# Row scatters from a queue, row numbers of y in a tile of their own, and an earlier place for the w1 loads of the first large visits

## The chip, the cores and the metric

The kernel runs on one core of a Trainium2 chip. The metric is the time of one execution on the device in microseconds (us). The engines are PE (matrix multiplication), DVE (VectorE), ACT (ScalarE), POOL (GpSimd) and SP (here only an issuer of DMAs). The DMA engines work beside them: SP's loads go through one queue, POOL's scatters through another.

## The reference

The first part is a convolution over the sequence (8 sequences of 2880 tokens, 192 channels) whose 7 weights are different for every token and head; they are the softmax of `weight_gen`. The second part sends each of the 23,040 tokens to one of 16 experts (4 groups of 4, the largest logit of each) and scales the expert's output by both softmax weights.

```python
w = np.exp(weight_gen - weight_gen.max(-1, keepdims=True))
w = w / (w.sum(-1, keepdims=True) + 1e-09)            # [B, S, 8 heads, 7]
x = np.einsum('bshk,bskhg->bshg', w, x_unf).reshape(N, 192)
g_idx = argmax(x @ w_group)                            # group, gate g_w from its softmax
e_idx = argmax(x @ w_expert[g_idx])                    # expert, gate e_w from its softmax
out[token] = g_w * e_w * (relu(x @ w1[g, e]) @ w2[g, e])   # 192 -> 1024 -> 192
```

## The kernel before

The tokens lie as 128 partitions x 180 columns. Fifteen column groups (g0 to g14) of twelve columns each go through three steps. The softmax (lines 258 to 263, on DVE and ACT) and the convolution (DVE products, some of the sums on PE) make the rows `xrow`; the tiles `wt` and `xin` that they read are loaded by `load_group` (lines 115 and 125). The routing (`logits` and `ranks`) finds each token's expert and its place in the expert's list, `posi`. Then, per group, twelve indirect DMAs on POOL (lines 480 to 482 and 488) scatter 128 rows each of 194 numbers (192 channels, the gate and the token's own number) to `rows` in DRAM, where every expert has a stretch of its own.

The experts' work goes by visits. A visit takes rows of one expert: 128 (plain), 256 (pair) or 384 (triple). Its inputs are `xb` (the rows, line 744), w1 and w2 (`wc`, line 768), all asked by SP. The first ten visits are plain and use float32 w1 as it is (`wa`, line 755). All others are large: w1 comes into `raw` tiles (512 KB at line 757, and 256 KB each from w1 and from `w1lo` at line 764), and ACT casts it into `wa` (lines 781 and 790), with a subtraction on DVE (line 805). `prep_d` (825 to 830) and `prep_x` make the visit's transposed inputs; `gemm1` (872) and the relu on ACT (878, 883) make the hidden layer, `gemm2` (910) the output, ACT scales it to `y` (919), and POOL scatters y's 128 rows to `out` by the token's numbers, which it reads from `xb` (927). In this kernel a visit's DMA on POOL therefore holds its xb buffer until it is done.

Fifteen rounds of visits follow the groups: a round may begin when the groups that it needs are scattered (the table `ENDS`: 2, 3, ... 15 groups), and the last one holds most triples. DVE's work for the next groups is a generator that the loop over visits advances (`fill`), by a planner's clocks for each engine. The order on PE, ACT, DVE and SP is that in which the program is written; POOL's order is left to the scheduler (line 101):

```python
ctx.enter_context(tc.manual_schedule(engines={ET.PE, ET.Activation, ET.DVE, ET.SP}))
```

In the loop of `blocks`, the inputs of later visits are asked (lines 1074 to 1077) at the last unit of a visit.

Of the kernel before, what the change touches and what calls it, by code (L numbers as in the profile page):

```python
# [11 lines left out]
I32 = mybir.dt.int32  # L12
# [8 lines left out]
LATE = (1.0, 3.0, 3.0)  # L21
AHEAD = (1.0, 1.0, 2.5)
HURRY = 12
WHOLE = 13
SINGLE = tuple((k,) for k in range(7))
MIXED = ((0, 1), (2,), (3,), (4,), (5,), (6,))
# [11 lines left out]
def conv_moe_kernel(ctx: ExitStack, tc: tile.TileContext, x, wgen, w_group, w_expert, w1, w2, out):  # L38
    nc = tc.nc
# [157 lines left out]
    def ring(name, n, shape, dt=F32):  # L197
        tiles = [const.tile(shape, dt, name=f"{name}{i}") for i in range(n)]
        at = [0]

        def take(i=None):
            at[0] += 1
            return tiles[(at[0] if i is None else i) % n]
        return take
# [3 lines left out]
    new_xh = ring("xh", 2, [P, 2, 3 * P], F32R)  # L208
    new_xl = ring("xl", 2, [P, 2, 3 * P], F32R)
    new_y = ring("y", 9, [P, D])  # L210
    hls = []

    def new_hl():
# [6 lines left out]

    new_raw = [ring(f"raw{i}", m, [P, n]) for i, (n, m) in enumerate(((F, 2), (F, 2), (NFT * D, 1)))]

    state = {"slots": False, "open": False, "unit": 0, "starve": False, "ph": 0, "hold": False}

    def ph_tile(k, shape):
        return ps_h.tile(shape, F32, name=f"ph{k}")
# [9 lines left out]
    def run(eng, cost, *deps):  # L236
        clk[eng] = max([clk[eng]] + [d + HOP for d in deps]) + cost
        return clk[eng]
# [10 lines left out]
    def round_of(g):  # L249
        return next(r for r in range(NR) if g < ENDS[r])  # L250
# [164 lines left out]
    def ranks(g, o, ls, tls):  # L415
# [61 lines left out]
        pi = rt.tile([P, SG], I32, name="posi", bufs=2)[:, 0:n]  # L477
        nc.vector.scalar_tensor_tensor(out=pi, in0=ps, scalar=-1.0, in1=ps, op0=ALU.mult, op1=ALU.max)
        yield TINY
        for s in range(n):  # L480
            run("pool", 1.28, clk["dve"])
            scatter_row(pi[:, s:s + 1], xrow[s // SC][:, s % SC, :], round_of(g))
        if g + 1 in ENDS:
            yield from table(round_of(g))
        o.routed = True

    def scatter_row(idx, src, r):
        written_once(nc.gpsimd.indirect_dma_start(  # L488
            out=rows[:, :], out_offset=bass.IndirectOffsetOnAxis(ap=idx, axis=0),
            in_=src, in_offset=None, bounds_check=NROW - 1, oob_is_err=False), r)  # L490
# [109 lines left out]
        for h in range(2):  # L600
            nc.gpsimd.dma_start(out=rows[NROW + h * BK:NROW + (h + 1) * BK, :].rearrange("(p t) c -> p t c", t=2), in_=pad2)

    scoring, ranking = [], []
    slow = [[halves(), None]]

    def front():
        side = []
        set_up()
        load_group(1)
        next(slow[0][0])  # L610
        yield from softmax(0)

        def pace(g):
            return 99 if g <= FIRST else HURRY if g < MAIN + 3 else 8 if g in ENDS else 2

        def beside(g, n):
            rush = g >= FIRST and not grp[FIRST - 1].routed
            if g >= FIRST and not rush:
                for q in list(slow):
                    yield from move(slow, q, 1)  # L620
            for q in side[:1]:
                if not rush:
                    yield from move(side, q, 3)
            yield from routing(g)

        def routing(g):
            if ranking:
                yield from move(ranking, ranking[0], pace(g))
            if scoring and (not ranking or g < FIRST):
                yield from move(scoring, scoring[0], pace(g) if scoring[0][2].chunks == 2 or g >= FIRST - 1 else 3)  # L630

        def settle(g):
            while not grp[g].routed:
                qs = ranking or scoring
                q = qs[0]
                yield from move(qs, q, 99)
                if qs and qs[0] is q and q[1] is not None:
                    yield Until(q[1][1]) if q[1][0] == "time" else NEXT

        for g in range(ENDS[-1]):  # L640
            o = grp[g]
            o.routed = False
            scoring.append([logits(g, o), None, o])
            for n, c in enumerate(conv(g, o)):
                yield c
                if n == (2 if state["slots"] else 0) and 1 <= g < ENDS[-1] - 1:
                    load_group(g + 1)
                if n >= (12 if state["slots"] else 4) and not o.ahead and g + 1 < ENDS[-1] and g != FIRST - 1:
                    o.ahead = True
                    side.append([softmax(g + 1), None])  # L650
                yield from beside(g, n)
                if g == FIRST - 1 and n in (7, 8):
                    if n == 7:
                        soft = softmax(FIRST)
                    yield next(soft)
            if g == FIRST - 1:
                for n, c in enumerate(soft):
                    yield c
                    yield from beside(g, n)
            yield from finish_all(side)  # L660
            if g:
                yield from settle(g - 1)
        yield from settle(ENDS[-1] - 1)
# [54 lines left out]
    nmain = len(order)  # L718

    def ready(n):  # L720
        return order[n][:2] in arrive

    def plain(n):
        return order[n][1] == 1
# [98 lines left out]
        latest.clear()  # L823

    def prep_d(b):
        if b.plain:
            return
        b.xd = new_xd()[:, 0:b.nt]
        b.td = run("act", 0.1 + 0.13 * b.nt, b.o.tx)
        nc.scalar.copy(out=b.xd, in_=b.x[:, :, P:D].unsqueeze(2).broadcast_to([P, b.nt, 2, HP]))  # L830
# [92 lines left out]
    def send(b, t, y):  # L923
        if not b.o.whole:
            nc.vector.scalar_tensor_tensor(
                out=y, in0=b.py[t][:, D:2 * D], scalar=b.x[:, t, D:D + 1], in1=y, op0=ALU.mult, op1=ALU.add)
        ins = nc.gpsimd.indirect_dma_start(  # L927
            out=out[:, :], out_offset=bass.IndirectOffsetOnAxis(ap=b.x.bitcast(I32)[:, t, D + 1:D + 2], axis=0),
            in_=y, in_offset=None, bounds_check=NTOK - 1, oob_is_err=False)
        tc.declare_no_dep(ins.ins, group="outw", reason="every token is written once")  # L930
        tc.add_to_no_dep_group("outw", ins.ins)

    def need(n):
        while not ready(n):
            state["starve"] = True
            more = step() is not False
            assert more or ready(n)
        state["starve"] = False
# [13 lines left out]
    def blocks(n0, n1, paced):  # L952
# [92 lines left out]
        for i in range(len(units) + LAG):  # L1045
# [25 lines left out]
            if i < len(units):  # L1071
                n, at = units[i]
                end = at == last
                if end and n + 3 < n1 and (plain(n + 3) or plain(n + 2)):
                    ask_w(n + 3)
                    if not plain(n + 3):
                        ask_w(n + 4)
                did = 0
                for job in list(jobs):
                    m, part, h = job  # L1080
                    if m > n + 2 or (part == 3 and (m > n + 1 or at < LAG)):
                        continue
                    must = end and m == n + 1
                    if not must and (did >= 1 or (m, part) in want or not ready(m)):
                        continue
                    jobs.remove(job)
                    work_split(job)
                    did += 1
                state["unit"] += 1
            flush()  # L1090
            if paced:
                fill(clk["pe"] + AHEAD[0 if cur.plain else 1 if cur.o.whole else 2])
# [48 lines left out]
```

## Time and profile before

| | |
|---|---|
| median of 3 runs | 1333.68 us (1323.01 to 1336.16) |
| the profiled execution | 1335.81 us |
| its span, first to last instruction | 1334.1 us |
| mean granted TensorE clock | 0.951 of full speed |
| busy | PE 89%, DVE 71%, ACT 48%, POOL 34% |

The time of an execution holds a little more than the span. Busy time is that of an engine's instructions; idle time has behind it, in the timeline, the instruction that ended it. "issue" is time in which the engine waited for nothing that the profile shows, and "remote" is a semaphore whose setter the profile doesn't tell. PEclk is the granted clock in a stretch, as a share of full speed (2.4 GHz; its other level is 1.2 GHz).

### The profile page before, as it was taken

To read this page: it belongs to the slowest core of one execution; us is meant where nothing else is said; L and a number is where in the kernel's file an instruction comes from. 1 tells how busy PE (TensorE), PEld (TensorE's weight loads), DVE (VectorE), ACT (ScalarE), POOL (GpSimd) and SP (SyncE) were. 2 spreads that over 40 slices of the span, in tenths; PEclk is the share of its full clock that TensorE was granted. 3 is DMA by queue.
4 is the path that set the end of the run, shared out by engine and by line. 5 is a ranking of instruction groups with operands and counts; after the bars stand their busy time and mean duration, and the time that the engine had idled before them with its cause. 6 is when DMAs were issued, how large, how long until landed. Compare 5 with 4: busy or idle time off the path is not lost. (4 is left out here: it accounts for less than half of the span.)

```text
span 1334.1 us, 23736 instructions
## 1 busy us (share of the span) xinstructions
PE 1192.9 (89%) x8165; PEld 1104.5 (83%) x8165; DVE 950.5 (71%) x1660; ACT 640.1 (48%) x1232; POOL 455.6 (34%) x442
## 2 busy tenths in 40 slices
PE   5776877798999999999989798989786999999995
PEld 3444877688998989898989697989686999999995
DVE  8897776768988979798978597888633146655662
ACT  1223334344555555455545454645343466556652
POOL 6232331415253525344533415252416312112221
PEclk9988998788999999899999899999887999999998
DMA  9238789555878767677776666545436665565551
GB/s 258 85 120 275 239 213 287 190 197 172 265 224 278 215 236 225 228 223 253 229 237 213 217 196 209 188 155 168 158 88 216 197 205 149 154 176 165 151 164 39
DMA packets 78851, 261.94 MB, mean 196 GB/s; under 512 B 14669, under 2 KB 29559, under 8 KB 76928
## 3 DMA queue, kind: packets, MB, share of 16 engines
q1 hardware_dynamic: 59544, 220.85, 54.4%
q0 software_dynamic: 19056, 39.20, 8.8%
q8 instruction: 66, 1.08, 0.3%
q14 instruction: 65, 0.53, 0.1%
q10 hardware_dynamic: 120, 0.28, 0.1%
HBM read 216.92 MB, written 44.23 MB: 196 GB/s over the span
## 5 line engine op out<-in xcount | busy, mean ns | idle before, releaser
L872 PE MATMUL ph<-xh,wa 128*128 128x256 f32 (+1 forms) x1896 | 477.0, 321 | 8.1 <-issue 7.4
L910 PE MATMUL py<-wc,hh 128*128 128x192 f32 x2272 | 440.2, 334 | 34.4 <-issue 17.5
L927 POOL DMA_INDIRECT out<-y,xb x189 | 222.1, 1175 | 706.3 <-ACT y L919 449.5
L910 PEld LDWEIGHTS py<-wc,hh 128*128 128x128 f32 x2272 | 379.2, 196 | 40.6 <-issue 22.3
L872 PE MATMUL ph<-xl,wa 128*128 128x256 f32 (+1 forms) x1264 | 360.4, 300 | 8.1 <-issue 8.1
L878 ACT ACTIVATE hh<-ph 128x512 f32<-128x512 f32 (+2 forms) x320 | 175.9, 550 | 366.5 <-PE ph L872 258.4
L872 PEld LDWEIGHTS ph<-xh,wa 128*128 128x128 f32 x1896 | 329.5, 194 | 17.9 <-issue 16.4
L488 POOL DMA_INDIRECT rows<-xrow,posi x180 | 202.1, 1123 | 152.6 <-issue 65.9
L287 DVE TENSOR_TENSOR pr<-xin,wt 128x1152 f32<-128x1152 f32 x186 | 249.0, 1351 | 4.3 <-PE ph L328 2.0
L872 PEld LDWEIGHTS ph<-xl,wa 128*128 128x128 f32 x1264 | 243.4, 193 | 9.5 <-issue 9.5
L305 DVE TENSOR_TENSOR xrow<-xrow,pr 128x1152 f32<-128x1152 f32 x144 | 194.9, 1353 | 0.6
L805 DVE TENSOR_TENSOR wa<-raw,wa 128x1024 fp32r<-128x1024 f32 x79 | 96.5, 1221 | 127.8 <-ACT wa L781 111.7
L805 DVE SCALAR_TENSOR_TENSOR pr<-ph,hh 128x384 fp32r<-128x384 f32 (+1 forms) x120 | 68.8, 574 | 89.0 <-ACT hh L883 84.0
L805 DVE TENSOR_TENSOR xl<-tpx,xh 128x512 fp32r<-128x512 f32 (+1 forms) x99 | 62.8, 634 | 61.5 <-ACT xh L852 50.6
L883 ACT ACTIVATE hh<-ph 128x384 fp32r<-128x384 f32 (+1 forms) x120 | 61.1, 510 | 79.8 <-PE ph L872 70.5
L912 PE MATMUL py<-wc,hh 128*128 128x384 f32 x272 | 87.2, 362 | 0.0
L781 ACT CAST wa<-raw 128x1024 fp32r<-128x1024 f32 x79 | 82.9, 1049 | 7.0 <-DMA raw<-in_moe_w 7.0
L790 ACT CAST wa<-raw 128x1024 fp32r<-128x1024 f32 x79 | 82.8, 1048 | 0.5 <-DMA raw<-w1lo 0.5
L919 ACT ACTIVATE y<-py,xb 128x192 f32<-128x192 f32 x176 | 66.2, 424 | 27.2 <-PE py L910 19.0
L391 ACT COPY xT<-tp 128x384 f32<-128x384 f32 x84 | 40.3, 480 | 78.3 <-PE pl L367 30.5
L913 PE MATMUL py<-wc,pr 128*128 128x192 f32 x272 | 68.4, 251 | 0.0
L852 ACT CAST xh<-tpx 128x512 fp32r<-128x512 f32 (+1 forms) x99 | 53.5, 540 | 3.9 <-PE py L910 1.8
(170 smaller groups left out, 1287.2 us busy)
## 6 DMA issues: line engine op xcount, KB each, us to landing
wc<-in_moe_w SPq DMA_DIRECT2D x73, 768.0 KB
raw<-in_moe_w SPq DMA_DIRECT2D x79, 512.0 KB
xin<-in_x SPq DMA_DIRECT2D x14, 1728.0 KB
raw<-in_moe_w SPq DMA_DIRECT2D x87, 256.0 KB
raw<-w1lo SPq DMA_DIRECT2D x79, 256.0 KB
raw<-in_moe_w SPq DMA_DIRECT2D x17, 768.0 KB
xb<-rows SPq DMA_DIRECT2D x59, 194.0 KB
wa<-in_moe_w SPq DMA_DIRECT2D x22, 384.0 KB
```

The lines of the kernel that those rows point to most:

```text
L287: nc.vector.tensor_tensor(out=dst, in0=o.xin[:, c0 + k:c0 + k + SC, :].rearrange("p s (h g) -> p s h g", g=HG), in1=w4[:, c0:c0 + SC, :, k ...
L305: nc.vector.tensor_tensor(out=acc, in0=acc, in1=prs[k - 2], op=ALU.add)
L488: written_once(nc.gpsimd.indirect_dma_start(out=rows[:, :], out_offset=bass.IndirectOffsetOnAxis(ap=idx, axis=0), in_=src, in_offset=None, ...
L781: nc.scalar.copy(out=o.wa[:, 0, :], in_=o.raw[0])
L790: nc.scalar.copy(out=o.wa[:, 2, :], in_=o.raw[1])
L805: f(*a, **k)
L872: nc.tensor.matmul(ph[:, v, :], lhsT=w[:, f0:f0 + P], rhs=rhs, start=i == 0, stop=i == len(terms) - 1)
L878: nc.scalar.activation(out=hh, in_=ph, func=AF.Relu)
L910: nc.tensor.matmul(b.acc[t], lhsT=hh[:, v, c], rhs=wc[0][:, f, :], start=f == 0 and not (b.wide and t == 1), stop=f == NFT - 1 and not (b. ...
L912: nc.tensor.matmul(b.py[t], lhsT=hh[:, v, c], rhs=wc[f // 4][:, f % 4].rearrange("p l d -> p (l d)"), start=f == 0, stop=False)
L913: nc.tensor.matmul(b.acc[t], lhsT=hl[:, v, c], rhs=wc[f // 4][:, f % 4, 0, :], start=False, stop=f == NFT - 1)
L927: ins = nc.gpsimd.indirect_dma_start(out=out[:, :], out_offset=bass.IndirectOffsetOnAxis(ap=b.x.bitcast(I32)[:, t, D + 1:D + 2], axis=0), ...
```

## The change

Three things are changed.

*The scatters of rows.* `ranks` no longer issues them, but puts them into a list, `sending`. `send_rows` takes them from it, and for the first groups does so at once. Otherwise the loop over visits issues one in each unit, if the planner's clock for PE is 3 us further (`send_due`). A group's rows are issued at the latest when the next but one is begun. A round counts as ready only when the rows of its groups are sent.

*The row numbers of y.* In `prep_d`, ACT copies the token's numbers of a visit from xb to a ring of six small tiles, `ids`, and the y scatter reads them from there.

*The asks of w1.* Of the first two large visits, w1 is asked two visits sooner.

```diff
+    new_ids = ring("ids", 6, [P, 3, 1], I32)
...
-        for s in range(n):
-            run("pool", 1.28, clk["dve"])
-            scatter_row(pi[:, s:s + 1], xrow[s // SC][:, s % SC, :], round_of(g))
+        sending.extend((g, pi[:, s:s + 1], xrow[s // SC][:, s % SC, :], s == n - 1, clk["dve"]) for s in range(n))
+        if g < FIRST:
+            send_rows()
...
+    def send_rows(most=99):
+        while sending and most > 0:
+            g, idx, src, end, at = sending.pop(0)
+            run("pool", 1.28, at)
+            scatter_row(idx, src, round_of(g))
+            most -= 1
+            if end:
+                state["sent"] = g + 1
+                for r, nb in arrive:
+                    if ENDS[r] == g + 1:
+                        arrive[r, nb] = max(arrive[r, nb], clk["pool"] + 7.0)
+    def send_due():
+        if sending and state["due"] <= clk["pe"]:
+            send_rows(1)
+            state["due"] = max(state["due"], clk["pe"] - 2.6) + GAP
...
         for g in range(ENDS[-1]):
+            while sending and sending[0][0] < g - 1:
+                send_rows(1)
...
-        return order[n][:2] in arrive
+        return order[n][:2] in arrive and state["sent"] >= ENDS[order[n][0]]
...
     def prep_d(b):
+        b.ids = new_ids()[:, 0:b.nt]
+        nc.scalar.copy(out=b.ids, in_=b.x.bitcast(I32)[:, :, D + 1:D + 2])
+        run("act", 0.22, b.o.tx)
...
-            out=out[:, :], out_offset=bass.IndirectOffsetOnAxis(ap=b.x.bitcast(I32)[:, t, D + 1:D + 2], axis=0),
+            out=out[:, :], out_offset=bass.IndirectOffsetOnAxis(ap=b.ids[:, t, :], axis=0),
...
-                if end and n + 3 < n1 and (plain(n + 3) or plain(n + 2)):
+                if end and n + 3 < n1 and plain(n + 3):
                     ask_w(n + 3)
-                    if not plain(n + 3):
-                        ask_w(n + 4)
+                if end and n + 6 < n1 and plain(n + 4) and not plain(n + 5):
+                    ask_w(n + 5)
+                    ask_w(n + 6)
...
+            send_due()
             flush()
```

POOL's order around the rows of one middle group, g11 (its row tiles are the `xrow` and `posi` here), before:

```order
L927 DMA out_0<-y7_188,xb2_174 23040x192
L927 DMA out_0<-y8_189,xb2_174 23040x192
L488 DMA rows_89<-xrow_7677,posi_9184 188928x194 x6
L488 DMA rows_89<-xrow_7678,posi_9184 188928x194 x6
L927 DMA out_0<-y0_181,xb0_172 23040x192
L927 DMA out_0<-y1_182,xb0_172 23040x192
```

The same group with the change:

```order
L951 DMA out_0<-y8_189,ids0_190 23040x192
L507 DMA rows_89<-xrow_7788,posi_9294 188928x194 x6
L507 DMA rows_89<-xrow_7789,posi_9294 188928x194 x4
L951 DMA out_0<-y0_181,ids1_191 23040x192
L951 DMA out_0<-y1_182,ids1_191 23040x192
L507 DMA rows_89<-xrow_7789,posi_9294 188928x194 x2
L951 DMA out_0<-y2_183,ids2_192 23040x192
```

The twelve scatters of the group are still in a row up to the tenth; two y scatters stand ahead of the last two. Of the thirteen groups from g2 on, g3, g6 and g8 are cut 7 and 5, g9 and g11 10 and 2, the others but the last not at all.

POOL's order at the last group, g14, before (line 541 loads a place for a padding block):

```order
L488 DMA rows_89<-xrow_10371,posi_11394 188928x194
L927 DMA out_0<-y0_181,xb2_174 23040x192
L927 DMA out_0<-y1_182,xb2_174 23040x192
L488 DMA rows_89<-xrow_10371,posi_11394 188928x194 x5
L488 DMA rows_89<-xrow_10372,posi_11394 188928x194 x6
L541 TENSOR_LOAD pfi_11471
```

With the change, in two pieces, the first up to the padding blocks and the second behind the last of them:

```order
L507 DMA rows_89<-xrow_10469,posi_11567 188928x194 x2
L951 DMA out_0<-y2_183,ids1_191 23040x192
L951 DMA out_0<-y3_184,ids1_191 23040x192
L507 DMA rows_89<-xrow_10469,posi_11567 188928x194 x3
L560 TENSOR_LOAD pfi_11614
```

```order
L562 DMA rows_89<-pad_169 256x1x194
L507 DMA rows_89<-xrow_10469,posi_11567 188928x194
L507 DMA rows_89<-xrow_10470,posi_11567 188928x194 x6
L951 DMA out_0<-y6_187,ids3_193 23040x192
L951 DMA out_0<-y7_188,ids3_193 23040x192
```

Seven of the twelve scatters now stand behind the sixteen padding blocks, among which (not shown) two more y scatters stand behind the seventh.

SP's order where the plain visits end, before (`wt` and `xin` are the next column group's, `xb0` and `wc` the last plain visit's, `raw00` is the first part of w1 of the first large visit; TENSOR_LOAD and ISA rows read and compute addresses):

```order
L115 DMA wt_1734<-in_weight_gen 128x672
L125 DMA xin_1736<-in_x 128x3456
L743 TENSOR_LOAD tab1_782
L743 ISA x2
L744 ISA
L744 DMA xb0_172<-rows_89 128x194
L768 ISA
L768 DMA wc_1808<-in_moe_w2 128x1536
L752 TENSOR_LOAD tab2_1382
L752 ISA x2
L757 ISA
L757 DMA raw00_190<-in_moe_w1 128x1024
```

With the change, from the second large visit's `raw` on:

```order
L778 DMA raw01_197<-in_moe_w1 128x1024
L785 ISA
L785 DMA raw11_199<-in_moe_w1 64x1024
L785 ISA
L785 DMA raw11_199<-w1lo_90 64x1024
L116 DMA wt_1773<-in_weight_gen 128x672
L126 DMA xin_1775<-in_x 128x3456
L764 TENSOR_LOAD tab1_788
L764 ISA x2
L765 ISA
L765 DMA xb0_172<-rows_89 128x194
L789 ISA
```

All six raw loads of two visits stood behind `wc` and now stand ahead of `wt`; `xb0` and `wc` keep their place behind `xin`.

## Rows read from the trace of the kernel before

**Rows 1.** Busy line of the page; windows: us, busy (x count) per engine, PEclk, DMA, GB/s.

```profile
PE 1192.9 (89%) x8165; PEld 1104.5 (83%) x8165; DVE 950.5 (71%) x1660; ACT 640.1 (48%) x1232; POOL 455.6 (34%) x442
...
231.00:1040.00 809.00, 742.49 (x5349) 705.99 (x5348) 619.26 (x1115) 405.55 (x765) 318.26 (x282) 0.95 0.66 209
1040.00:1330.00 290.00, 279.62 (x1843) 273.07 (x1841) 149.27 (x251) 166.76 (x322) 60.77 (x59) 0.99 0.53 154
0.00:231.00 231.00, 170.81 (x977) 125.46 (x978) 181.95 (x295) 67.81 (x146) 76.60 (x102) 0.93 0.71 211
```

**Rows 2.** Windows of 28 us around twelve runs of scatters: two, and the sum.

```profile
726.00:754.00 28.00, 19.11 (x121) 17.84 (x120) 14.70 (x29) 9.88 (x20) 16.18 (x16) 0.82 0.51 157
...
996.00:1024.00 28.00, 17.88 (x102) 16.56 (x101) 12.43 (x63) 7.45 (x14) 19.79 (x21) 0.77 0.54 168
sum 336.00, PE 276.08 PEld 255.85 DVE 244.41 ACT 144.64 POOL 212.46; mean PE 23.01 PEld 21.32 DVE 20.37 ACT 12.05 POOL 17.70
```

**Rows 3.** Twelve windows of 28 us between the runs: one, and the sum.

```profile
756.00:784.00 28.00, 28.00 (x241) 26.74 (x240) 25.24 (x32) 16.57 (x31) 4.73 (x4) 1.00 0.80 269
...
sum 336.00, PE 335.42 PEld 324.61 DVE 255.08 ACT 199.29 POOL 71.20; mean PE 27.95 PEld 27.05 DVE 21.26 ACT 16.61 POOL 5.93
```

**Rows 4.** Timeline of POOL: start, us, engine line op out<-in xcount [idle before <-releaser].

```profile
726.14 0.97 POOL L488 DMA_INDIRECT rows<-xrow,posi  x1 [5.89 <-DVE units L514]
...
740.23 0.97 POOL L488 DMA_INDIRECT rows<-xrow,posi  x1 [0.30 <-issue]
...
751.18 1.86 POOL L927 DMA_INDIRECT out<-y,xb  x1 [7.41 <-ACT y L919]
```

**Rows 5.** Timeline of PE and ACT at that run; ACT's waits over the span.

```profile
740.55 0.48 PE L910 MATMUL py<-wc,hh 128*128 128x192 f32 x1 [1.65 <-issue]
...
746.29 1.09 ACT L878 ACTIVATE hh<-ph 128x512 f32<-128x512 f32 x2 [15.24 <-remote]
...
ACT hh L878 <- remote: 76.9, 14, 15.2
```

**Rows 6.** Waits from 840 to 1100: us in total, times, longest.

```profile
SPq L744 <- DMA out<-y,xb: 140.6, 14, 25.7
...
ACT xd L830 <- DMA xb<-rows: 7.2, 6, 1.6
...
PE tpx L846 <- DMA xb<-rows: 3.4, 3, 3.0
```

**Rows 7.** Smallest ACT operation of the routing: durations in ns, min/median/max.

```profile
L345 ACT ACTIVATE exe<-de x15: 233/240/243, 50.2 to 993.2; 128x48 f32<-128x48 f32 x15
```

**Rows 8.** Timeline of SP's queue where the plain visits end.

```profile
194.98 0.38 SPq L115 DMA_DIRECT2D wt<-in_weight_gen  x1
...
198.35 0.33 SPq L757 DMA_DIRECT2D raw<-in_moe_w  x1
```

**Rows 9.** Timelines of DVE, ACT and PE behind these loads.

```profile
204.59 0.85 DVE L258 TENSOR_REDUCE m<-wt 128x96 f32<-128x672 f32 x1 [5.79 <-DMA wt<-in_weight_gen]
...
206.37 0.76 ACT L261 ACTIVATE wt<-wt 128x672 f32<-128x672 f32 x1 [1.54 <-DVE wt L260]
207.04 0.64 ACT L878 ACTIVATE hh<-ph 128x256 f32<-128x256 f32 x2
...
216.06 1.04 ACT L781 CAST wa<-raw 128x1024 fp32r<-128x1024 f32 x1 [7.02 <-DMA raw<-in_moe_w]
...
218.01 1.65 PE L910 MATMUL py<-wc,hh 128*128 128x192 f32 x4 [6.08 <-ACT y L919]
```

**Rows 10.** Windows over the same stretch.

```profile
204.00:210.00 6.00, 6.00 (x47) 5.77 (x48) 5.30 (x7) 2.05 (x5) 0.00 (x0) 1.00 1.02 373
210.00:216.00 6.00, 1.93 (x16) 1.74 (x14) 2.81 (x10) 0.00 (x0) 0.00 (x0) 1.00 1.03 202
216.00:226.00 10.00, 7.99 (x44) 7.99 (x45) 6.61 (x14) 6.11 (x14) 0.97 (x1) 0.66 1.03 275
```

More of the change, by code (lines that the diff above doesn't have):

```diff
@@ L23 @@
 HURRY = 12
+GAP = 3.0
 WHOLE = 13
@@ L221, in conv_moe_kernel @@
     new_raw = [ring(f"raw{i}", m, [P, n]) for i, (n, m) in enumerate(((F, 2), (F, 2), (NFT * D, 1)))]
-    state = {"slots": False, "open": False, "unit": 0, "starve": False, "ph": 0, "hold": False}
+    state = {"slots": False, "open": False, "unit": 0, "starve": False, "ph": 0, "hold": False, "sent": 0, "due": 0.0}
     def ph_tile(k, shape):
@@ L601, in set_up @@
             nc.gpsimd.dma_start(out=rows[NROW + h * BK:NROW + (h + 1) * BK, :].rearrange("(p t) c -> p t c", t=2), in_=pad2)
-    scoring, ranking = [], []
+    scoring, ranking, sending = [], [], []
     slow = [[halves(), None]]
@@ L934, in need @@
         while not ready(n):
+            send_rows()
+            if ready(n):
+                break
             state["starve"] = True
```

## The prediction

> **What bounds the kernel now.** I read the busy times first. PE works 1192.9 us of 1334.1 [rows 1], so 141 us of its time are open, and no other engine comes near it. Then I read the windows, to see where these 141 us lie. Up to 231 us PE has 170.81 us of work, which leaves 60.2 us open while the first rows are made and the plain visits run; from 231 to 1040 it has 742.49 of 809, which leaves 66.5; behind 1040 it has 279.62 of 290 [rows 1]. The middle stretch holds almost all that can be won: 66.5 us of idle time and a granted clock of 0.95, which is another 0.05 x 809 = 40 us of full-speed work.
>
> The middle stretch is not evenly loose. I cut twelve windows of 28 us around the runs of twelve row scatters and twelve of the same length between them. The calm ones have 335.42 us of PE work in 336, the ones with a run have 276.08 [rows 2, 3]. So the runs cost 335.42 - 276.08 = 59.3 of the 66.5 us, and the clock falls in them too (0.82 and 0.77 in two of the worst, 1.00 in a calm one). That is 59.3 / 12 = 4.9 us of idle time and 40 / 12 = 3.3 us of clock for each run.
>
> The timeline shows how a run does it. POOL issues twelve scatters 1.28 us apart, from 726.14 to 740.23 [rows 4]. Towards its end PE's matmuls come one by one with 1.65 us between them and wait for nothing that the profile names ("issue"), and ACT stands 15.24 us for a "remote" semaphore before the next relu [rows 5]; over the span ACT stands so 76.9 us in 14 places [rows 5]. It is not the bandwidth: the DMA share is 0.51 and 0.54 in two of the worst windows and 0.80 in the calm one [rows 2, 3]. What exactly is starved in PE's supply the trace does not tell; that it follows the runs of scatters it tells in every one of the twelve windows.
>
> **The change part by part.**
>
> **a) Scatters from a queue.** Issued one by one with 3 us between them, they would take the twelve back-to-back issues apart, which is where 59.3 + 40 = 99.3 us lie. But POOL's order is not the order in which the program is written: it is left to the scheduler, and the rows of the order show the scatters in runs again. Seven of the thirteen groups from g2 on still stand as twelve in a row; g3, g6 and g8 are cut 7 and 5, g9 and g11 10 and 2, each by two y scatters. Nothing in POOL's new program waits for the 3 us: no new wait is on a scatter. A cut alone is worth little, because the last group was cut 1 and 11 before and its window (996 to 1024) is the worst of all, with 28 - 17.88 = 10.1 us idle and 0.23 x 28 = 6.4 us of clock [rows 2]. So I put the twelve earlier groups at 0. Only the last group is truly taken apart: 2, then 3, then seven of the padding blocks, two y scatters, the other nine padding blocks, and the last 7. For it I take half of 10.1 + 6.4 = 16.5, which is **-8**. Bounds: 0, if the last 7 scatters cost what twelve did, and -99 if all runs were really thinned.
>
> **b) Row numbers for y in a tile of their own.** The y scatters no longer read xb, so a load into an xb buffer need not wait for them. SP stood 140.6 us for this in 14 places between 840 and 1100 [rows 6], which looks large, but SP is asked far ahead: in the same stretch PE waits 3.4 us for rows and ACT 7.2 [rows 6]. I take PE's **-3.4**; bounds 0 (the rows' scatters may be what is late next, since the load waits for those as well) and -3.4 - 7.2 = -10.6.
>
> **c) The copies.** One copy of at most 128 x 3 numbers for each of 90 visits on ACT. No copy so small stands in the trace; the nearest row is an activation of 128 x 48 at 0.240 us [rows 7], so at most 90 x 0.240 = 21.6 us of an engine that works 640.1 of 1334.1 us [rows 1]. They lie in front of the copy for the next visit that ACT does anyhow, with one visit of time ahead of them. Only in the plain stage does the copy stand a little earlier than the one that waited for xb, and there a relu is queued behind it. I take **+2**, a tenth; bounds 0 and +21.6 (if ACT's relus were always the last thing PE waits for, which rows 3 speak against: PE is full there).
>
> **d) w1 of the first large visits.** The order shows six w1 loads, 2 x (512 + 256 + 256) KB = 2.10 MB, moved ahead of wt and xin of the next column group, and ahead of xb and w2 of the last plain visit. SP issues them only from about 195 instead of 198.35 [rows 8]; the DMA engines have a share above 1.0 from 204 to 216 [rows 10], so this is an exchange of places in a full queue and not a gain of two visits. What comes sooner: before, ACT stood for raw to 216.06, and PE for 6.08 us behind that, until 218.01 [rows 9]. What comes later: wt, which landed at 204.59 and then released the softmax's maximum on DVE [rows 9]. Behind it are exp on ACT at 206.37 and, in ACT's order, the plain relu at 207.04 [rows 9]. With 2.10 MB ahead, at the 202 GB/s of the stretch in which mostly w1 arrived [rows 10], wt lands 10.4 us later, at 215.0, and the relu goes at 217.4 instead of 207.04. PE's stand of 6.08 us moves from behind to ahead of it and grows: 10.4 - 6.1 = **+4.3**. Bounds: -9.5, if the stand simply goes (6.1 us, and 0.34 x 10 = 3.4 us of the clock of 0.66 from 216 to 226 [rows 10]), and +10.4 if the old stand stays too.
>
> The sign of d) rests on who is served first. wt was asked at 194.98 and had landed by 204.59, raw was asked at 198.35 and landed by 216.06 [rows 8, 9]: in the order of asking. The Trainium skill (page DMA: Bandwidth & Descriptors, section Queues, rings and completion order) says that on each DMA engine the descriptors of a ring are consumed in ring order, while completions need not follow it. By that rule alone the exchange costs +4.3 and the forecast's sum holds; were transfers of one queue served side by side, it would be near -9.5.
>
> **Sum**, against the profiled execution of 1335.8: -8 - 3.4 + 2 + 4.3 = -5.1, which gives 1330.7. The median of the runs shown is 1333.7, 2.1 lower, so the forecast is **1329**.
>
> **The rivals.**
>
> *The runs are thinned after all.* Where a y scatter stands in a run, POOL stops for that y: 7.41 us in one place [rows 4]. If such stops let PE's supply recover in the cut groups, and later emission pulls the others apart too, half of the 99.3 us comes back: 1335.8 - 49.7 - 3.4 + 2 + 4.3 = 1289.0, as a median 1287. For it: the calm windows. Against it: seven groups uncut, and the cut last group of before being the worst. 0.16.
>
> *The w1 wait goes and the last run costs nothing.* 1335.8 - 9.5 - 16.5 - 3.4 + 2 = 1308.4, as a median 1306. For it: the stand behind raw is the largest single one at that place. Against it: wt, whose delay must then be hidden, though a relu is queued behind its exp. 0.18.
>
> *Slower: ACT stands behind wt.* The six loads hold wt back by 10.4 us, and the stand behind w1 does not go away, since w2 and xb of the last plain visit come behind xin: 128 x 3456 numbers, 1.77 MB, at 202 instead of 373 GB/s [rows 10] is another 8.8 - 4.7 = 4.1 us; PE then stands twice, which costs the half clock of 216 to 226 once more, 3.4; the last run costs what it did. 1335.8 + 10.4 + 4.1 + 3.4 + 2 - 3.4 = 1352.3, as a median 1350. It decides if wt lands behind about 215 with the relu queued behind its exp. For it: the DMA share above 1.0. Against it: DVE and ACT may have other work there, as PE had (6.00 of 6 us from 204 to 210). 0.18.
>
> *The change does nothing that can be seen*: scatters in runs, SP's waits hidden, the exchange of places neutral: 1334. It is one of the cases within 1%.
>
> **How the numbers follow.** A measurement of this kernel can tell about 1% from no change, that is 1320 to 1347. The forecast has 0.33 and the case of no effect 0.15, both within: same 0.48. Faster is 0.16 + 0.18 = 0.34, slower 0.18. The range reaches down to 1300, which takes in the second rival and leaves out most of the first, and up to 1351, which takes in the slower one: about 0.8 is inside. The forecast's own range, within its bounds, is 1320 to 1340.
>
> **What would show it.** a) In the profile after, the windows around runs of scatters should have the same 23.0 us of PE in 28 as before, with "issue" ahead of the matmuls, and only the last run less idle time; if the runs are still twelve long and PE is full in them, the link between runs and idle time is wrong. b) SP's waits for "out" should be gone and PE's waits for rows below 4 us. c) 90 copies of about 0.2 us, with PE's work in calm windows unchanged. d) wt should land near 215 and the plain relu near 217, and ACT should no longer stand for raw. A median under 1320 would say that the runs or the w1 wait went; one above 1347 that d) was mis-sized.

## The result and the profile after

The changed kernel takes 1347.85 us (median of 15 runs, 1333.14 to 1351.99), the kernel before beside it 1330.58 us (15 runs, 1323.01 to 1336.16). The ratio is 1.0118, with an interval of 1.009 to 1.0147: some 16 us slower by the ratio and 17.3 by the medians, where 1329 us and no change beyond 1% were forecast. The time lies in the stated range, and on the wrong side of before.

The profiled execution of after has a span of 1347.8 us, 13.7 more than before. The busy line of its page and two windows (in us: length, busy time and count of PE, PEld, DVE, ACT and POOL, then the granted clock, the DMA share and GB/s), as in [rows 1]:

```profile
PE 1189.4 (88%) x8165; PEld 1104.6 (82%) x8165; DVE 948.5 (70%) x1660; ACT 648.9 (48%) x1322; POOL 444.7 (33%) x442
...
0.00:231.00 231.00, 170.67 (x940) 124.06 (x941) 176.41 (x281) 66.67 (x153) 70.23 (x101) 0.90 0.66 203
231.00:1040.00 809.00, 728.63 (x5333) 696.99 (x5332) 621.17 (x1119) 410.16 (x822) 297.81 (x263) 0.94 0.65 206
```

PE works 3.5 us less than before and stands 1347.8 - 1189.4 = 158.4 us, against 141.2 [rows 1]: 17.2 more, and 17.2 - 3.5 is the 13.7 of the span. Up to 231 us the idle time is the same (60.3 us open, 60.2 before), but PE has done 940 matmuls where it had done 977, at a clock of 0.90 instead of 0.93, and the same y scatter starts 4.9 us later (the first line is before, the second after):

```profile
227.04 0.97 POOL L927 DMA_INDIRECT out<-y,xb  x1 [7.83 <-ACT y L919]
231.96 1.15 POOL L951 DMA_INDIRECT out<-y,ids  x1 [5.64 <-ACT y L943]
```

By 293 us most of this delay is gone: ACT's y there goes at 293.56, 1.8 us behind the 291.79 of before. From 231 to 1040 PE stands 80.4 instead of 66.5 us.

Windows of 28 us around the runs of scatters, as in [rows 2], now thirteen of them since the last group is in two pieces; three of the worst, and the sum:

```profile
307.00:335.00 28.00, 19.92 (x115) 19.13 (x113) 14.70 (x33) 8.71 (x17) 14.50 (x14) 0.82 0.65 200
399.00:427.00 28.00, 17.21 (x107) 16.55 (x106) 15.10 (x28) 7.69 (x15) 14.43 (x15) 0.76 0.55 171
...
681.00:709.00 28.00, 19.39 (x117) 18.26 (x117) 15.79 (x32) 10.84 (x22) 17.12 (x16) 0.76 0.49 159
...
sum 364.00, PE 287.01 PEld 271.29 DVE 220.83 ACT 142.81 POOL 216.44; mean PE 22.08 PEld 20.87 DVE 16.99 ACT 10.99 POOL 16.65
```

They lose 364 - 287.0 = 77.0 us. The twelve of before lost 336 - 276.08 = 59.9 [rows 2]. The 17.1 us between them are all of the idle time that was added. Group by group it goes both ways: the run at 399 lost 9.3 us more than the same group's in before, that at 307 lost 4.3 more (8.1 against 3.8), and the group that lost 8.9 us at 726 in before [rows 2] loses 3.0 in after, at 758. The run of before that belongs to the one at 399 began at 385.7 us and lost little, in its window:

```profile
385.00:413.00 28.00, 26.50 (x201) 25.05 (x201) 22.80 (x39) 14.75 (x28) 18.73 (x16) 1.00 0.81 261
```

The timelines of after at that run, POOL, then PE, then ACT (start, length, engine, line, what it does, and the idle time ahead of it with what ended it):

```profile
399.69 1.04 POOL L507 DMA_INDIRECT rows<-xrow,posi  x1 [0.30 <-issue]
...
413.83 0.97 POOL L507 DMA_INDIRECT rows<-xrow,posi  x1 [0.30 <-issue]
...
405.68 0.37 PE L896 MATMUL ph<-xl,wa 128*128 128x256 f32 x1 [0.42 <-issue]
407.06 0.27 PE L870 MATMUL tpx<-ident,xb 128*128 128x128 f32 x1 [1.01 <-issue]
416.68 0.47 PE L871 MATMUL tpx<-ident,xd 128*128 128x128 f32 x1 [9.35 <-ACT xd L854]
...
415.65 0.60 ACT L902 ACTIVATE hh<-ph 128x512 f32<-128x512 f32 x1 [13.56 <-remote]
416.14 0.18 ACT L848 COPY ids<-xb 128x2 int32<-128x2 int32 x1
416.22 0.41 ACT L854 COPY xd<-xb 128x256 f32<-128x256 f32 x1
```

PE's last `ph` matmul has ended at 406.05 at the latest, and ACT starts the relu at 415.65, when the run of scatters is over. Behind that relu, in ACT's order, stands the copy `xd` that PE's next transpose (for the visit that comes next) reads, and PE takes its work in the order of the program, so that it stands 9.35 us. Over the span, the waits of after (us in total, times, longest):

```profile
ACT hh L902 <- remote: 96.7, 19, 13.6
...
PE tpx L871 <- ACT xd L854: 28.5, 5, 9.4
```

The first was 76.9 us in 14 places [rows 5]. The second is new; in the waits of before it is this row:

```profile
PE tpx L847 <- ACT xd L830: 0.3, 2, 0.2
```

The late start of relus while a run is on is there before and after. What is new is what PE has in front of it: in five runs of after it is the transposes for the next visit, and the five waits fall in five of the thirteen windows (9.35, 5.71, 2.92, 7.14 and 3.36 us). This is not all that makes a run dear: the runs of before that lost 8.9 and 10.1 us in the windows of [rows 2] had no such wait.

### The profile page after: what moved, and what is told of

It reads as the page before. It is cut to its first block, busy times and chain, and to the rows that moved or that the text cites. A ratio compares the mean times of both kernels' runs of the same rounds, so it can differ in the third digit from the quotient of the medians.

```text
span 1347.8 us, 23695 instructions
## 1 busy us (share of the span) xinstructions
PE 1189.4 (88%) x8165; PEld 1104.6 (82%) x8165; DVE 948.5 (70%) x1660; ACT 648.9 (48%) x1322; POOL 444.7 (33%) x442
## 2 busy tenths in 40 slices
DMA packets 78851, 261.94 MB, mean 194 GB/s; under 512 B 14669, under 2 KB 29559, under 8 KB 76928
## 4 chain that ended last, share of the span: by engine, by line
PE 61%; issue 17%; another core or an unknown queue 6%; DVE 6%; POOL 4%; ACT 3%; DMA 1%; SPq 0%; POOLq 0%; ACTq 0%; DVEq 0%
PE py L934 26%; PE ph L896 25%; POOL out L951 3%; DVE pr L289 3%; PE pl L369 2%; PE tp L386 1%; PE tpx L871 1%; PE ph L330 1%; PE tpx L870 1%; DMA wt<-in_weight_gen 1%; PE py L330 1%; PE tp L387 1%; ACT xT L393 1%; DVE xrow L307 1%
## 5 line engine op out<-in xcount | busy, mean ns | idle before, releaser
L951 POOL DMA_INDIRECT out<-y,ids x189 | 215.4, 1140 | 744.6 <-ACT y L943 493.1
L896 PE MATMUL ph<-xl,wa 128*128 128x256 f32 (+1 forms) x1264 | 355.8, 298 | 7.0 <-issue 7.0
L896 PEld LDWEIGHTS ph<-xh,wa 128*128 128x128 f32 x1896 | 328.8, 193 | 16.7 <-issue 15.2
L507 POOL DMA_INDIRECT rows<-xrow,posi x180 | 197.7, 1098 | 136.6 <-issue 67.1
L871 PE MATMUL tpx<-ident,xd 128*128 128x128 f32 x178 | 47.8, 290 | 39.8 <-ACT xd L854 28.5
L393 ACT COPY xT<-tp 128x384 f32<-128x384 f32 x84 | 40.4, 481 | 67.3 <-PE pl L369 28.5
```

The lines of the kernel that those rows point to most:

```text
L507: written_once(nc.gpsimd.indirect_dma_start(out=rows[:, :], out_offset=bass.IndirectOffsetOnAxis(ap=idx, axis=0), in_=src, in_offset=None, ...
L896: nc.tensor.matmul(ph[:, v, :], lhsT=w[:, f0:f0 + P], rhs=rhs, start=i == 0, stop=i == len(terms) - 1)
L951: ins = nc.gpsimd.indirect_dma_start(out=out[:, :], out_offset=bass.IndirectOffsetOnAxis(ap=b.ids[:, t, :], axis=0), in_=y, in_offset=None ...
```

## Experiments

The record gives the chip of each experiment by a number: 8 for the second run of the row numbers, 1 for the last experiment, 7 for all others. It gives none for the comparison above. On all three numbered chips the kernel before takes 1247 us, not 1331. Below, "the first chip" is that of the comparison and "the second" stands for the numbered ones; that the chip is what differs, and not something else at that time, is not shown.

**The kernel before, once more.**

> The kernel before, unchanged, for a trace from the same chip as the runs beside it: it took 1246.9 us beside the first four experiments and 1330.6 beside the changed kernel, and the traces of the experiments have no matmuls that trickle behind the runs of scatters. Theory A (that trickle is what is between 1247 and 1331, and it belongs to the chip or its state and not to the program): a time near 1247 comes with full PE in the runs' windows, a time near 1331 with 59 us of idle time in them. Theory B (both times come with the same idle time in those windows): the difference lies elsewhere, for instance in the clock.

1248.8 us. Two of the twelve windows around its runs, the sum of the twelve, and two longer stretches:

```profile
356.00:384.00 28.00, 28.00 (x220) 27.57 (x219) 26.17 (x43) 17.67 (x33) 20.29 (x17) 1.00 0.86 274
419.00:447.00 28.00, 28.00 (x219) 27.55 (x219) 26.09 (x40) 16.08 (x30) 18.61 (x16) 1.00 0.86 254
...
sum 336.00, PE 314.17 PEld 304.62 DVE 289.27 ACT 182.35 POOL 221.99; mean PE 26.18 PEld 25.39 DVE 24.11 ACT 15.20 POOL 18.50
...
220.00:800.00 580.00, 573.38 (x4433) 557.05 (x4430) 523.54 (x855) 332.61 (x620) 239.07 (x207) 0.99 0.77 244
800.00:960.00 160.00, 140.37 (x949) 134.49 (x948) 95.08 (x252) 75.54 (x153) 74.68 (x76) 0.96 0.59 181
```

In seven of the twelve windows PE is full at full clock, with twelve scatters 1.28 us apart. No "remote" stands in ACT's waits and no "issue" in PE's. All twelve together lose 336 - 314.17 = 21.8 us, where they lost 59.9 on the first chip. So 38 of these 59.9 us do not come with the program wherever it runs; theory A. Of the 87 us between the two spans, 50 are idle time of PE (91.0 us here against 141.2) and 37 longer work of PE (1156.2 against 1192.9), at a mean clock of 0.974 for 0.951.

The two traces of the comparison differ from those of the experiments in one more thing: their record of semaphores has gaps (13,691 and 13,412 events in all, against 18,673 in this one), and they tell no landing of most loads. Of the w2 loads, before on the first chip and then here:

```profile
wc<-in_moe_w SPq DMA_DIRECT2D x73, 768.0 KB
wc<-in_moe_w SPq DMA_DIRECT2D x73, 768.0 KB, 7.6
```

So "remote" and "issue" of the first chip are readings of an incomplete record. Whether the gaps and the stalls have one cause is open.

What is left on PE on this chip lies for the most part from 800 to 960, and has a name, in the waits of PE and of SP's queue and in PE's timeline:

```profile
PE tpx L846 <- DMA xb<-rows: 16.3, 5, 10.5
...
SPq L744 <- DMA out<-y,xb: 299.3, 32, 23.0
...
939.56 0.45 PE L846 MATMUL tpx<-ident,xb 128*128 128x128 f32 x1 [10.49 <-DMA xb<-rows]
```

And the timelines of POOL and SP show why the rows come so late:

```profile
914.45 0.97 POOL L488 DMA_INDIRECT rows<-xrow,posi  x1 [0.31 <-issue]
...
927.38 0.97 POOL L488 DMA_INDIRECT rows<-xrow,posi  x1 [0.30 <-issue]
928.34 2.22 POOL L543 DMA_DIRECT2D rows<-pad  x3
931.42 1.04 POOL L927 DMA_INDIRECT out<-y,xb  x1 [0.86 <-issue]
...
935.35 0.34 SPq L744 DMA_DIRECT2D xb<-rows  x1
```

A y scatter stands behind the run, it still reads xb, SP may not load new rows into that xb before it is done and asks for them at 935.35, and PE gets them at 939.56.

**The changed kernel, once more.**

> The changed kernel, unchanged, beside before on this chip. Where the runs of scatters don't hold PE back, the parts alone gave +8.7 us (asks), -22.6 (row numbers) and -7.6 (queue). Theory A (the parts add, and the slowing by 1.2% came from where the runs fall on a chip on which they hold PE back): 1247 - 21 = about 1225, ratio 0.983. Theory B (the change is slower by itself): ratio 1.01 again. On a chip where before takes 1331, A expects 1.01 and a new layout of the stalls.

1226.98 against 1246.73 us: ratio 0.9832 (0.9803 to 0.986). On this chip the change is faster by 1.7%; theory A, to 2 us of its sum.

**Row numbers alone.**

```diff
-            out=out[:, :], out_offset=bass.IndirectOffsetOnAxis(ap=b.x.bitcast(I32)[:, t, D + 1:D + 2], axis=0),
+            out=out[:, :], out_offset=bass.IndirectOffsetOnAxis(ap=b.ids[:, t, :], axis=0),
```

with the ring and the copy in `prep_d`.

> The kernel before with the row numbers of y copied to a tile of their own, alone. Forecast by its own terms: -3.4 us of waits for rows and +2 for the copies, about 1329. Rival (the copy stands in ACT's queue ahead of relus and waits for xb, 9.0 us in 4 places in the trace of after): +9, about 1340. A third theory: SP's loads start sooner (140.6 us of waits for out end), so the transfers collide in another way with the runs of scatters, and the time moves by up to 10 us either way without a wait of its own to show for it.

1224.3 us, ratio 0.9821 (0.9795 to 0.9847): -22.6 us, by none of the theories' numbers; that of the third, up to 10, has the right mechanism in part. The stretch from 800 to 960, where before has 140.37 us of PE work:

```profile
800.00:960.00 160.00, 155.60 (x1090) 151.35 (x1089) 95.37 (x251) 86.89 (x183) 78.02 (x81) 1.00 0.66 207
```

15.2 us of work more in the same time, at a clock of 1.00 instead of 0.96. Over the span PE stands 17.7 us less than in before (73.3 against 91.0) and its work takes 7.5 us less (1148.7 against 1156.2). The same kernel a second time:

> Row numbers alone once more, to see whether another chip shows what the first comparison showed. Where before takes about 1247: 1224 again. Where it takes about 1331, theory A (runs of scatters hold PE back there, and where a run falls in a visit decides how long): a time anywhere from 1300 to 1345, with stalls named issue and remote; theory B (the row numbers bring the same everywhere): 1331 - 23 = 1308.

It came to a further chip, number 8, on which before takes 1246.6 us, and took 1226.4 us, ratio 0.9841 (0.9812 to 0.9869): the same gain again, and no "remote" in its waits. What the row numbers bring where before takes 1331 stays open.

**The copies alone.** The y scatters read xb again, and nobody reads the copies (the cut shows the step from the run of the row numbers alone).

```diff
-            out=out[:, :], out_offset=bass.IndirectOffsetOnAxis(ap=b.ids[:, t, :], axis=0),
+            out=out[:, :], out_offset=bass.IndirectOffsetOnAxis(ap=b.x.bitcast(I32)[:, t, D + 1:D + 2], axis=0),
```

> The kernel before with the 90 copies of row numbers on ACT, which nobody reads: the y scatters read xb as before. It measures the copies alone. Theory A (they lie in ACT's idle time): 0 to +2 us. Theory B (each delays the relu behind it): up to 90 x 0.18 = +16 us. The difference to row numbers alone (-22.6) is what the earlier release of xb brings.

1249.1 against 1248.4, ratio 1.0012 (0.9991 to 1.0033). One copy takes 0.185 us in the trace, and 90 of them cost nothing that can be told from 0; theory A. The 22 us are therefore the earlier release of xb.

```profile
L828 ACT COPY ids<-xb x90: 182/185/196, 115.8 to 1216.0; 128x2 int32<-128x2 int32 x59, 128x3 int32<-128x3 int32 x20, 128x1 int32<-128x1 int32 x11
```

They are not free everywhere, though. In the plain stage a copy waits for xb ahead of the routing's work and of the next relu. The same two relus of before, and then with the copies:

```profile
168.87 0.39 ACT L878 ACTIVATE hh<-ph 128x256 f32<-128x256 f32 x1 [1.16 <-PE ph L872]
...
173.97 0.38 ACT L878 ACTIVATE hh<-ph 128x256 f32<-128x256 f32 x1 [0.56 <-PE ph L872]
...
165.95 0.39 ACT L882 ACTIVATE hh<-ph 128x256 f32<-128x256 f32 x1 [1.16 <-PE ph L876]
169.72 0.19 ACT L828 COPY ids<-xb 128x1 int32<-128x1 int32 x1 [3.38 <-DMA xb<-rows]
...
176.85 0.38 ACT L882 ACTIVATE hh<-ph 128x256 f32<-128x256 f32 x1 [1.47 <-PE ph L876]
```

That is 10.9 us between them instead of 5.1. Later visits take it back.

**The asks of w1 alone.**

```diff
-                if end and n + 3 < n1 and (plain(n + 3) or plain(n + 2)):
+                if end and n + 3 < n1 and plain(n + 3):
                     ask_w(n + 3)
-                    if not plain(n + 3):
-                        ask_w(n + 4)
+                if end and n + 6 < n1 and plain(n + 4) and not plain(n + 5):
+                    ask_w(n + 5)
+                    ask_w(n + 6)
```

> The kernel before with the w1 asks moved alone. In the traces of before and after, the visits behind the first large one are 4.9 us later in after (y number 6 at 198 us), and this edit is the only one that moves anything there. Theory A (the exchange of places in SP's queue costs what it showed and is not given back): +5 us, about 1335. Theory B (the slack of the later stages takes it back, and the loss of after comes from the scatters alone): 0, about 1330. Theory C (the asks are the whole loss): +17, about 1347.

1255.55 us, ratio 1.0066 (1.0041 to 1.0091), +8.7 us; nearest to theory A. The 4.9 us of its expectation are not the asks' alone, as it says: the y scatters number 4 to 8 (counted from 0) start 3.3 to 6.9 us later than in before with the row numbers alone, and with the asks alone only those from number 6 on, by 7.9 to 10.3. PE's timeline has the price in one place, a plain visit whose rows stand in the queue behind the six w1 loads:

```profile
196.00 0.66 PE L837 MATMUL tp<-ident,xb 128*96 128x128 f32 x2 [9.87 <-DMA xb<-rows]
```

**Row numbers and asks.** The diffs of the two experiments above together, and the scatters as in the kernel before.

> Row numbers and asks, without the queue. Theory A (parts add): 1247 - 22.6 + 8.7 = 1233. Theory B (the queue is what pays in the changed kernel, or what harms it): differs from the changed kernel by the queue's part, 7.6 us, up or down.

**Row numbers and queue.** The changed kernel with the asks' diff taken back.

> The changed kernel with the old asks of w1, so row numbers and queue alone. Theory A (parts add): 1247 - 22.6 - 7.6 = 1217, that is 8.7 us below the changed kernel. Theory B (row numbers and queue remove the same waits for rows): about 1224, as the row numbers alone. If the asks cost nothing beside the other two: the same as the changed kernel.

Row numbers and asks: 1230.98 us, ratio 0.9874 (0.9846 to 0.9901), near theory A's 1233. Row numbers and queue: 1222.53 us, ratio 0.9801 (0.9774 to 0.9828), nearer to theory B's 1224 than to 1217. The asks cost 6.7 us beside the row numbers alone (1230.98 - 1224.3) and 4.5 in the changed kernel (1226.98 - 1222.53). Without them the kernel has the lowest time of all on this chip, clearly below before; its interval overlaps that of the changed kernel. It was not timed on the first chip.

**The queue alone.** `sending`, `send_rows` and `send_due` as in the change, y scatters from xb and the old asks.

> The kernel before with the scatters put through the list, alone; w1 asks and row numbers as before. Theory A (the runs stay and fall on other places of PE's and ACT's work, where they hold them longer: in after 'remote' of ACT is 96.7 us against 76.9): +8 to +12 us, about 1340. Theory B (the queue changes nothing that counts): 0. Theory C (thinning helps and the other parts lose): below 1325.

1239.3 us, ratio 0.994 (0.9918 to 0.9962): -7.6 us, the sign of theory C, with a smaller size. PE's longest wait for rows falls from 10.5 to 2.9 us:

```profile
PE tpx L866 <- DMA xb<-rows: 11.4, 8, 2.9
```

Beside the row numbers the queue brings 1.8 us (1222.5 against 1224.3), within their intervals: it shortens the waits that the row numbers remove.

**A real pause between the scatters.**

```diff
+            one = rt.tile([P, 1], I32, name="one", bufs=2)
+            nc.gpsimd.tensor_copy(out=one, in_=pi[:, s:s + 1])
-            scatter_row(pi[:, s:s + 1], xrow[s // SC][:, s % SC, :], round_of(g))
+            scatter_row(one, xrow[s // SC][:, s % SC, :], round_of(g))
```

> The kernel before, but with a real pause between the row scatters on POOL: each scatter reads its row numbers from a tile of one column of which there are two, filled by a copy on POOL, so that a copy waits until the scatter two before it is done. Theory A (it is the back-to-back issue of twelve that holds PE's and ACT's semaphores and instructions back: 59.3 us of idle time and about 40 us of clock): the runs' windows have PE work near 27.9 in 28 and the time falls by 50 to 99 us, to 1230 to 1280. Rival B (the sum of the scatters' work holds PE back, however it is spaced): the same idle time spread wider, about 1330. Rival C (the pauses hold y's scatters and the next rounds back): slower, 1340 or more.

1312.62 us, ratio 1.0517 (1.0483 to 1.0551); rival C, and the gain that I had put at up to 99 us had nothing to come from on this chip. POOL stands for a scatter to land, its y scatters and the next rounds' rows come later, and PE waits for rows:

```profile
POOL one L483 <- DMA rows<-xrow,one: 122.6, 61, 5.6
...
PE tpx L848 <- DMA xb<-rows: 42.3, 11, 17.8
```

**Every row scatter twice**, the second time into a spare tensor; the result does not use it.

```diff
+            if g >= 2:
+                ins = nc.gpsimd.indirect_dma_start(
+                    out=rows2[:, :], out_offset=bass.IndirectOffsetOnAxis(ap=pi[:, s:s + 1], axis=0),
+                    in_=xrow[s // SC][:, s % SC, :], in_offset=None, bounds_check=NROW - 1, oob_is_err=False)
```

> The kernel before, with each row scatter from g2 on issued twice, the second time into a spare tensor that nobody reads: runs of 24 instead of 12, 156 more scatters of 1.28 us (200 us of POOL). Theory A (a run of scatters holds PE's instructions and semaphores back by itself, the longer the more): the runs' windows lose twice the work, +60 us of idle time and more on a chip where before takes 1331, and stalls named issue and remote appear on a chip where it takes 1247. Theory B (on a chip where before takes 1247 a run costs nothing on PE, however long): no such stalls; the time grows only where POOL's y scatters and the rows of the next rounds come later, by 15 us for each run that is on the path: between +5 and +60 us, with PE waiting for rows by name.

1304.99 us, ratio 1.0447 (1.041 to 1.0485). A window over a run of 24, and the waits for rows:

```profile
364.00:402.00 38.00, 38.00 (x307) 36.91 (x306) 34.94 (x49) 23.00 (x43) 29.55 (x26) 1.00 0.83 268
...
PE tpx L853 <- DMA xb<-rows: 49.5, 7, 22.7
```

Theory B: no run holds PE's instructions back here, not one of 24, and no "issue" stands in PE's waits. Of the 56.6 us, 37.3 are named waits of PE for rows (49.5 and 8.9 in the large and the plain visits, against 16.3 and 4.8); 16.9 are PE's waits for ACT's `rem` (25.5 against 8.6), a copy that stands in ACT's order behind one that waits for rows; and PE's work takes 8.3 us more, at a mean clock of 0.952 for 0.974.

**The same, with the row numbers in a tile of their own:** the two diffs together.

> Every row scatter from g2 on twice, as in the doubled run, but with the row numbers of y in a tile of their own. With the doubled runs before took 1305.0 (+56.6), with 49.5 us of PE waiting for rows. Theory A (a run costs because y scatters stand behind it on POOL, and the xb that they hold lets the next rows start late): with the row numbers out of xb PE's waits for rows fall below 15 us and most of the 56.6 goes: 1235 to 1265. Theory B (the rows themselves come late, since the next round's scatters stand behind the doubled ones): 1305 - 23 = 1282, with PE still waiting some 30 us and more for rows.

1232.09 us, ratio 0.9884 (0.9852 to 0.9915). It ran on chip 1, where before takes 1247.2 us. Of the 56.6 us that the doubled scatters cost, 7.8 are left (1232.1 against 1224.3), and PE's wait for rows in the large visits is 3.5 us:

```profile
PE tpx L857 <- DMA xb<-rows: 3.5, 3, 2.1
```

Theory A, with a time 3 us under its range: a run costs, on these chips, because y scatters stand behind it on POOL and hold xb.

## Why the prediction was wrong

**What bounds the kernel.** On the chip of the comparison the reading holds: the runs of scatters are where PE stands, before (59.9 us) and after (77.0). But I took this for a property of the program. The second chip runs the same program with full PE in seven of the twelve, at 1247 us.

**a) The scatters: the step that failed.** The forecast that they stay in runs was right. "So I put the twelve earlier groups at 0" was not: it takes the price of a run as fixed, while the windows of before say that it goes from 1.5 us (385 to 413) to 10.1 (996 to 1024 [rows 2]). The groups begin at other times in after, and in five runs PE then had the next visit's transposes in front of it and waited 28.5 us for `xd` behind ACT's delayed relu. The windows of the earlier groups lost 69.6 us instead of 49.8, that is +19.8 where 0 was forecast. The whole term was +17.1 us of idle time instead of -8; the last group gained in its own windows (24.37 and 24.28 us of PE work in 28, where it had 17.88 [rows 2]):

```profile
1024.00:1052.00 28.00, 24.37 (x143) 23.84 (x142) 13.00 (x63) 12.70 (x24) 19.23 (x22) 0.94 0.96 299
1056.00:1084.00 28.00, 24.28 (x143) 23.81 (x142) 1.92 (x2) 9.94 (x20) 13.14 (x14) 0.88 0.64 192
```

That is 10.1 us before against 3.6 + 3.7 = 7.3 after. With the clock counted as in the forecast (0.06 x 28 + 0.12 x 28 = 5.0 us, where it was 6.4) it is 12.3 against 16.5, so -4.2 for the -8. No rival had this case: the slower one put the loss at w1. That the transposes for the next visit made these runs dear is read from the five waits and was not tried, since no experiment met these stalls. Which of the three edits moved the runs on the first chip stays open for the same reason, as does what delays the relus and PE's matmuls during a run.

**b) The release of xb.** On the first chip nothing contradicts -3.4: SP's waits for `out` (249.6 us over the span before) are gone from the trace, and PE had hardly waited for rows [rows 6]: over the span 8.0 us in before and 4.1 in after, so -3.9 (the edit was not run alone on that chip). On the second chip the same edit is worth 22.6 us. There PE, not held back by the runs, gets to the rows before they are there: before waits 21.1 us for them. My bound of -10.6 came from the waits that ended last on one chip; a wait that is hidden behind another is not bounded by its row.

**c) The copies.** +2 was forecast, 0.0012 x 1248 = 1.5 us measured, not to be told from 0. The size was right, and so was the place that it named: in the plain stage the copy waits for xb with a relu queued behind it. In after the two relus around such a copy are 8.26 us apart (180.01 and 188.27), where before had 5.10.

**d) w1.** The times came out as forecast on the first chip, in part by luck. DVE's maximum waits for wt until 215.35 (215.0 forecast), the relu goes at 217.80 (217.4), ACT no longer stands for raw, and PE's stand has moved behind the exp:

```profile
215.35 0.85 DVE L260 TENSOR_REDUCE m<-wt 128x96 f32<-128x672 f32 x1 [15.55 <-DMA wt<-in_weight_gen]
...
217.80 0.64 ACT L902 ACTIVATE hh<-ph 128x256 f32<-128x256 f32 x2
...
218.22 2.07 PE L896 MATMUL ph<-xd,wa 96*128 96x128 f32 x8 [5.84 <-ACT hh L902]
```

It did not grow, though: 5.84 us for 6.08 [rows 9].

The luck is in how wt came to be late. The forecast had six w1 loads of 2.10 MB go out from about 195 us and hold it back by 10.4 us; they went out from 200.53. In the trace wt took 10.4 us from its ask to its landing (204.93 to 215.35), and in before 9.6 (194.98 to 204.59 [rows 8, 9]): 0.8 more. It was late because it was asked 9.95 us later. SP's w1 loads for a plain visit, just ahead of this place, went out 4.9 us late already (before, then after):

```profile
194.02 0.86 SPq L755 DMA_DIRECT2D wa<-in_moe_w  x2
198.87 0.86 SPq L776 DMA_DIRECT2D wa<-in_moe_w  x2
```

The other 5.1 us are between these and wt, where SP now issues the six loads. The 4.9 us are a delay of the plain visits from about 185 us on, for which the forecast had no term at this place; on the second chip the copies of c) make such a delay by themselves.

On the second chip the asks cost 4.5 us in the changed kernel (+4.3 forecast) and 8.7 alone. The Trainium skill (page DMA: Bandwidth & Descriptors, section Queues, rings and completion order) says that on each DMA engine the descriptors of a ring are consumed in ring order, though a later one may finish before an earlier one. This trace does not contradict it, with wt asked at 204.93 behind the last raw load and landed by 215.35; as it tells no landing of the raw loads, it does not show it either.

```profile
204.36 0.47 SPq L785 DMA_DIRECT2D raw<-w1lo  x1
204.93 0.53 SPq L116 DMA_DIRECT2D wt<-in_weight_gen  x1
```

## What to carry to other kernels

Where a DMA's completion frees a buffer for a load, let it hold no more than it needs: 90 copies of 0.185 us took the y scatters off xb and were worth 22 us where PE had come to wait for rows, and made the kernel nearly deaf to doubled scatters (7.8 us instead of 56.6). A load that is asked sooner in a full queue changes places with others (here it cost 4.5 to 8.7 us), so price what it passes. And a stall whose length goes from 1.5 to 10 us between like places is no constant: a change that moves it, though it leaves it as it is, needs its own range, on both sides.

## What was not expected of the hardware

The same kernel took 1330.6 us in the comparison and 1246.7 beside the changed kernel on chip 7, 6.7% apart, with the same DMA traffic (261.94 MB in 78,851 packets). In the first, while twelve scatters are issued 1.28 us apart, a relu started 9.6 us behind PE's last matmul for it, and matmuls followed each other with 1.65 us between them [rows 5]; on the second chip PE was full beside 24. Of the change itself, the comparison says 1.0118 and chip 7 says 0.9832, and neither interval holds 1. What differs between the two is not known.
